# The first weight load of a decode block, issued in two parts

## Chip, cores and metric

One core of one Trainium2 chip. The metric is the device time of one execution in microseconds; the median of three runs of the kernel before is 264.27 us (264.25 to 264.36).

## The reference

One token for each of 8 sequences goes through a transformer block of width 1024, all in float32: layer norm, attention with 32 query heads on 4 key/value heads of size 128 over the last 1024 cached positions, output projection and residual; then layer norm, a gated feed-forward layer (3584 wide, gelu) and residual.

```python
def _A_ref(x, k_cache, v_cache, wq, wo):
    W = min(4096, max(256, Sk // 4))          # 1024
    q = (x @ wq).reshape(B, Sq, Hq, Dh).transpose(0, 2, 1, 3)
    k = jnp.repeat(k_cache[:, :, Sk - W:, :], rep, axis=1)
    v = jnp.repeat(v_cache[:, :, Sk - W:, :], rep, axis=1)
    p = _softmax(jnp.einsum("bhqd,bhkd->bhqk", q, k) * (Dh ** -0.5), axis=-1)
    o = jnp.einsum("bhqk,bhkd->bhqd", p, v)
    return o.transpose(0, 2, 1, 3).reshape(B, Sq, Hq * Dh) @ wo

def _B_ref(x, w_gate, w_up, w_down):
    h = _gelu(jnp.einsum("bsd,df->bsf", x, w_gate)) * jnp.einsum("bsd,df->bsf", x, w_up)
    return jnp.einsum("bsf,fd->bsd", h, w_down)

h = x + _A_ref(_layernorm(x), k_cache, v_cache, wq, wo)
h2 = h + _B_ref(_layernorm(h), w_gate, w_up, w_down)
```

## The kernel before

Weights and cache windows, 111 MB in all, lie in memory in the order of their use, each piece as 128 rows of equal length that are one contiguous stretch. They pass through two buffers in SBUF, `wbuf[0]` and `wbuf[1]`, of 128 x 16384 float32 each (64 KB a row, 8 MB a buffer). The first eleven loads fill a whole buffer in turn: two halves of wq, two of the keys, two of the values, two of wo, then gate and up. Smaller pieces follow: three of 4 MB, two of 2 MB, and a tail of 1 MB, 512 KB and two of 256 KB.

`load(k)` (its DMA is line 186) issues load k on SyncE's queue; its completion adds 16 to the semaphore of its buffer, `landed[0]` or `landed[1]`. Loads 0 and 1 are issued at the start without a wait, load 0 being the first half of wq. Between them ScalarE issues the DMA of x (line 191), 16 rows of 2 KB, which waits only for GpSimd's memset of its tile. Each later load waits until TensorE has done the last products on its buffer. The tail's four loads go through `move` (line 83).

TensorE runs a loop of stages that is written ahead of everything else. In a stage it takes the semaphore `turn` (the wait in `take` is line 127), makes eight transposes of the tile `tin` (line 132), then takes `landed[i]` and `ready[i]` and makes 32 products in two halves with the buffer's weights (line 146), the left side being the small tile `st[i]`. `turn` and `ready` are raised by the engines that make these tiles. Ahead of the loop it sets a register and branches to the stage; it waits for nothing there.

The first stage needs: x landed, the layer norm on VectorE and ScalarE (lines 221 to 233), eight transposes, two copies on VectorE (line 241), and a fill of each `st` on VectorE and GpSimd (line 246); and for its products load 0. After the last stage TensorE makes the down projection's last blocks from the tail (lines 450, 463 and 478), the result is copied (lines 482 and 483) and two DMAs carry it out.

All semaphores made through `Flow.sem` are cleared at the end by SyncE, as one range.

Of the kernel before, what the change touches and what calls it, by code (L numbers as in the profile page):

```python
# [10 lines left out]
D = 1024  # L11
# [79 lines left out]
def decode_block(nc, x, flow, tail, outs):  # L91

    fl = Flow(nc)
# [10 lines left out]
    wbuf = [space[:, i * BUF:(i + 1) * BUF] for i in range(2)]  # L104
# [7 lines left out]
    landed = [fl.sem("wa"), fl.sem("wb")]  # L112
    ready = [fl.sem("ga"), fl.sem("gb")]
    turn = fl.sem("turn")
    steps = fl.sem("steps")
    pace = fl.sem("pace")


    def pe(it, step):
# [3 lines left out]
    t = nc.tensor  # L123
# [29 lines left out]
        ins.then_inc(steps, 1)  # L153

    t.reg_mov(count, 0)
    t.br("stage")
    with nc.body("stage", valid_engines=[PE]):
        back = t.mark_branch_hint_location()
# [23 lines left out]
    def load(k, *waits):  # L182
        i, a, src, own = flow[k]
        n = src.shape[1]
        s = fl.sem(f"part{k}") if own else landed[i]
        fl.start("sync", lambda e: e.dma_start(wbuf[i][:, a:a + n], src), waits).then_inc(s, 16)
        return s, 16

    load(0)
    x_in = fl.sem("x")  # L190
    fl.start("scalar", lambda e: e.dma_start(xh[0:64:CP, :], x), [x_zero]).then_inc(x_in, 16)
    x_in = x_in, 16
# [95 lines left out]
    for hf in range(2):  # L288
# [16 lines left out]
        for k, engine in ((0, "vector"), (1, "scalar")):  # L305
            src = tp[:, k * N:(k + 1) * N].rearrange("p (c j m) -> p j c m", c=4, j=NQ)
# [7 lines left out]
    for hf in range(2):  # L314
# [17 lines left out]
        for s in range(2):  # L332
            src = tp[:, 64 * s:64 * s + 64].rearrange("p (b h) -> p h b", h=REP)
# [60 lines left out]
    for k in range(2, len(flow)):  # L394
        i, a, src, mine = flow[k]
# [37 lines left out]
    c0 = 0  # L433
# [133 lines left out]
```

## Time and profile before

| | |
|---|---|
| median of 3 runs | 264.27 us |
| the profiled execution's own time | 264.18 us |
| its span, first to last instruction | 262.9 us |
| weights' DMA queue, share of 16 engines' span | 98.3% |
| TensorE busy | 153.1 us (58%) |
| VectorE, ScalarE, GpSimd busy | 35.0, 16.5, 15.8 us |
| memory read | 111.18 MB, 423 GB/s over the span |
| x, issue to landing | 9.4 us |

The profile is one execution. All times in it are microseconds from the first instruction, so that the span is 1.3 us shorter than the time of the same execution. A DMA is cut into packets, here one for each row, shared out among 16 DMA engines; each engine ends its part of a DMA with a small write (under 512 B) to the DMA's semaphore, which the profile counts as a packet too. A packet belongs to the stretch in which it starts, with its whole duration, so that a short stretch can show more than 100% of its time.

### The profile page before, as it was taken

What the parts mean: (1) busy time and instruction counts of PE and PEld (TensorE: products, weight loads), DVE (VectorE), ACT (ScalarE), POOL (GpSimd) and SP (SyncE); (2) the same over time, 40 slices, a digit from 0 to 9 for tenths busy, and PEclk for the clock granted to TensorE, in tenths of its full rate; (3) what the DMA queues carried; (4) which work ended last, traced back from release to release, by engine and by line L of the source; (5) the groups of instructions that cost most, each with busy time, mean ns of one, the idle gap of its engine ahead of it and who ended that gap; (6) DMA issues with size and microseconds to landing.
All of it is one profiled execution on the core that took longest, in us unless ns stands there. A gap on an engine that the chain in (4) does not pass through costs nothing. (4 is left out here: it accounts for less than half of the span.)

```text
span 262.9 us, 2330 instructions
## 1 busy us (share of the span) xinstructions
PE 153.1 (58%) x992; PEld 51.6 (20%) x992; DVE 35.0 (13%) x79; ACT 16.5 (6%) x25; POOL 15.8 (6%) x31
## 2 busy tenths in 40 slices
PE   0024945816926617937728908529919509966696
PEld 0021221211211112212212202122212202312112
DVE  0220010000030110040220010730011300131012
ACT  1000000000040110000000000200200000010000
POOL 5020010010000000010020000020000200001000
PEclk9999995986995975975956995955977956999799
DMA  8998997999899899989999997999999799999995
GB/s 319 484 449 349 479 479 329 469 479 449 349 479 479 369 429 479 449 349 479 479 399 399 479 459 339 479 479 399 399 479 479 319 464 414 439 439 399 431 419 207
DMA packets 3200, 111.31 MB, mean 423 GB/s; under 512 B 368, under 2 KB 624, under 8 KB 1024
## 3 DMA queue, kind: packets, MB, share of 16 engines
q1 hardware_dynamic: 3024, 111.22, 98.3%
q10 hardware_dynamic: 176, 0.10, 0.1%
HBM read 111.18 MB, written 0.13 MB: 423 GB/s over the span
## 5 line engine op out<-in xcount | busy, mean ns | idle before, releaser
L146 PE MATMUL big<-w,st 128*32 128x512 f32 x832 | 133.9, 728 | 72.9 <-PEq L127 69.6
L146 PEld LDWEIGHTS big<-w,st 128*32 128x32 f32 x832 | 36.7, 130 | 161.9 <-issue 159.4
L132 PE MATMUL tp<-ident,tin 128*128 128x128 f32 x104 | 16.7, 312 | 34.2 <-PEq L127 34.2
L132 PEld LDWEIGHTS tp<-ident,tin 128*128 128x128 f32 x104 | 13.2, 159 | 44.5 <-issue 44.5
L255 POOL COPY st<-ot 128x256 f32<-128x256 f32 x8 | 2.9, 402 | 77.6 <-DVE ot L334 77.6
L293 DVE TENSOR_REDUCE nmax<-big 128x1 f32<-128x1024 f32 x2 | 2.4, 1224 | 29.9 <-PE big L146 29.9
L246 POOL COPY st<-xt 128x1024 f32<-128x1024 f32 x2 | 3.0, 1524 | 51.7 <-DVE xt L241 51.7
L271 DVE TENSOR_TENSOR tin<-big,q 128x512 f32<-128x512 f32 x2 | 1.4, 692 | 32.3 <-PE big L146 32.3
L319 DVE TENSOR_TENSOR o<-big,o 128x512 f32<-128x512 f32 x2 | 1.4, 692 | 30.7 <-PE big L146 30.7
L281 POOL COPY st<-qz 128x1280 f32<-128x1280 f32 x2 | 2.5, 1256 | 35.1 <-DVE qz L276 35.1
L255 POOL COPY st<-at 128x256 f32<-128x256 f32 x6 | 2.6, 466 | 31.5 <-DMA w<-weights 25.5
L270 ACT COPY q<-big 128x512 f32<-128x512 f32 x2 | 1.2, 586 | 35.5 <-PE big L146 35.5
L443 DVE TENSOR_TENSOR d<-big,d 128x512 f32<-128x512 f32 x2 | 1.4, 692 | 14.9 <-PE big L146 14.9
L405 DVE TENSOR_TENSOR gs<-big,gs 128x512 f32<-128x512 f32 x1 | 0.7, 692 | 19.1 <-PE big L146 19.1
L318 ACT COPY o<-big 128x512 f32<-128x512 f32 x2 | 1.2, 586 | 31.5 <-PE big L146 31.5
L255 POOL COPY st<-xt 128x256 f32<-128x256 f32 x2 | 1.3, 661 | 30.1 <-DVE us L377 30.1
L295 ACT ACTIVATE tin<-big,nmax 128x1024 f32<-128x1024 f32 x2 | 2.2, 1114 | 12.8 <-DVE nmax L293 12.8
L295 ACT ACT_TABLE_LOAD x1 | 1.3, 1283 | 25.1 <-DVE nmax L293 25.1
L348 DVE TENSOR_TENSOR y<-big,y 128x512 f32<-128x512 f32 x1 | 0.7, 692 | 16.1 <-PE big L146 16.1
L226 ACT ACT_TABLE_LOAD x2 | 2.6, 1283 | 1.9 <-POOL ident L197 1.9
L373 DVE TENSOR_TENSOR gs<-big,gs 128x512 f32<-128x512 f32 x1 | 0.7, 692 | 14.7 <-PE big L146 14.7
L404 ACT COPY gs<-big 128x512 f32<-128x512 f32 x1 | 0.6, 586 | 30.6 <-PE big L146 30.6
(75 smaller groups left out, 44.6 us busy)
## 6 DMA issues: line engine op xcount, KB each, us to landing
w<-weights SPq DMA_DIRECT2D x3, 4096.0 KB, 22.8
w<-weights SPq DMA_DIRECT2D x2, 2048.0 KB, 23.8
w<-weights SPq DMA_DIRECT2D x1, 1024.0 KB, 24.3
w<-weights SPq DMA_DIRECT2D x1, 512.0 KB, 25.2
w<-weights SPq DMA_DIRECT2D x2, 256.0 KB, 25.5
w<-weights SPq DMA_DIRECT2D x11, 27.3
out<-o_fin SPq DMA_DIRECT2D x1, 64.0 KB, 1.6
out<-o_fin ACTq DMA_DIRECT2D x1, 64.0 KB, 1.6
```

The lines of the kernel that those rows point to most:

```text
L132: ins = t.transpose(tp[:, i * P:(i + 1) * P], tin[:, i * P:(i + 1) * P], ident)
L146: ins = t.matmul(out[32 * j:32 * j + 32, :], st[i][:, s0:s0 + 32], wbuf[i][:, w0:w0 + N], start=(c == 0), stop=(c == 3))
L226: tok = run("scalar", lambda e: e.activation(sd, ve, AF.Sqrt), tok)
L246: fill = run(engine, lambda e: e.tensor_copy(windows(i), half.unsqueeze(2).to_broadcast([P, 2, NQ, 4 * 32])), tok, *clear)
L255: tok = run(engine, lambda e: e.tensor_copy(windows(i)[:, k, 2 * e2:2 * e2 + 2].rearrange("p h (c m) -> p h c m", m=32), s[:, e2].unsqueez ...
L270: tok = run("scalar", lambda e: e.copy(q_sb, w0), pe(0, ("a0", "b0")[hf]))
L271: tok = run("vector", lambda e: e.tensor_add(tin[:, 0:N], w1, q_sb), tok, pe(0, end), pe(0, ("t0", "t1")[hf]))
L281: fill = run("gpsimd", lambda e: e.tensor_copy(st[hf].rearrange("p (k n) -> p k n", k=2), qz[hf].unsqueeze(1).to_broadcast([P, 2, NQ * WIN ...
L293: tok = run("vector", lambda e: e.tensor_reduce(out=nmax, in_=s_ps, axis=AX.X, op=ALU.max, negate=True), pe(1, ("a1", "b1")[hf]))
L295: p_ok = run("scalar", lambda e: e.activation(tin, s_ps, AF.Exp, bias=nmax, accum_out=tot), tok, pe(1, ("t0", "t1")[hf]))
L319: tok = run("vector", lambda e: e.tensor_add(o_sb, big[hf][:, N:2 * N], o1), tok, pe(2, ("a1", "b1")[hf]))
L443: tok = run("vector", lambda e: e.tensor_add(d0, ya[:, k], d0), tok, pe(6, f"a{k}"))
```

## The change

Load 0 is issued as two DMAs on SyncE's queue. The first carries the first 1024 float32 (4 KB) of each of the 128 rows and signals a new semaphore, `first`; the second carries the other 60 KB of each row and signals `landed[0]`, as the whole load did. TensorE waits once for `first`, ahead of its branch into the stages. All else stays.

```diff
@@ -114,6 +114,7 @@
     pace = fl.sem("pace")
+    first = fl.sem("first")
@@ -153,6 +154,7 @@
     t.reg_mov(count, 0)
+    t.wait_ge(first, 16)
     t.br("stage")
@@ -186,7 +188,10 @@
-    load(0)
+
+    i, a, src, _ = flow[0]
+    for (c0, c1), s in (((0, D), first), ((D, src.shape[1]), landed[i])):
+        nc.sync.dma_start(wbuf[i][:, a + c0:a + c1], src[:, c0:c1]).then_inc(s, 16)
     x_in = fl.sem("x")
```

## Rows read from the trace of the kernel before

**Rows 1.** The page: span, busy tenths of the DMA engines in 40 slices, the weights' queue (packets, MB, share).

```profile
span 262.9 us, 2330 instructions
...
DMA  8998997999899899989999997999999799999995
...
q1 hardware_dynamic: 3024, 111.22, 98.3%
```

**Rows 2.** The chain that ended last, its end: start us, us, what.

```profile
233.38 0.33 SPq L83
...
233.76 25.23 DMA w<-weights
...
259.03 0.42 PE acc L463 x8
...
260.96 0.27 ACT o_fin L482
```

**Rows 3.** SyncE's waits (total us, times, longest); issues of loads 2 and 10.

```profile
SPq L186 <- PE big L146: 222.9, 12, 33.1
...
L186 SPq DMA_DIRECT2D w<-weights x1: 327/327/327, 34.7 to 34.7; - x1
...
L186 SPq DMA_DIRECT2D w<-weights x1: 327/327/327, 190.7 to 190.7; - x1
```

**Rows 4.** Packets starting in 41.15 to 41.68 us and 195.89 to 196.46 us.

```profile
DMA packets 32, 1.05 MB, mean 1979 GB/s; under 512 B 16, under 2 KB 16, under 8 KB 16
...
DMA packets 32, 1.05 MB, mean 1840 GB/s; under 512 B 16, under 2 KB 16, under 8 KB 16
```

**Rows 5.** The timeline of the first 24 us: start us, us, what [idle before].

```profile
0.74 0.85 SPq L186 DMA_DIRECT2D w<-weights  x2
...
1.28 0.57 ACTq L191 DMA_DIRECT2D xh<-x  x1
...
10.68 0.69 DVE L221 BATCH_NORM_STATS2 ln_bn<-xh 64x6 f32<-64x512 f32 x1 [8.60 <-DMA xh<-x]
...
14.06 1.94 PE L132 MATMUL tp<-ident,tin 128*128 128x128 f32 x8 [14.06 <-PEq L127]
...
16.59 1.56 POOL L246 COPY st<-xt 128x1024 f32<-128x1024 f32 x1 [12.50 <-DVE xt L241]
...
23.03 7.54 PE L146 MATMUL big<-w,st 128*32 128x512 f32 x40 [7.04 <-PEq L127]
```

**Rows 6.** DMA in 1.70 to 2.95 us (40 slices; queue), then 4.80 to 5.40 us.

```profile
GB/s 0 4194 6291 0 2097 8389 0 2097 2097 2097 2097 0 0 0 0 0 0 0 0 0 2097 0 0 0 0 0 0 0 0 0 0 0 0 0 0 0 0 0 0 2097
...
q1 hardware_dynamic: 16, 1.05, 245.9%
...
q1 hardware_dynamic: 16, 1.05, 403.1%
```

**Rows 7.** ScalarE's DMA queue in 7.20 to 7.80 us, then in 9.74 to 10.26 us.

```profile
q10 hardware_dynamic: 16, 0.03, 14.0%
...
q10 hardware_dynamic: 16, 0.00, 1.7%
```

**Rows 8.** The weights' queue in 100 to 117 us and in 257.22 to 257.94 us.

```profile
q1 hardware_dynamic: 112, 7.34, 99.7%
...
q1 hardware_dynamic: 71, 0.29, 100.0%
```

**Rows 9.** Packets starting in 256.66 to 257.23 us and 257.94 to 258.49 us.

```profile
DMA packets 63, 0.21 MB, mean 367 GB/s; under 512 B 16, under 2 KB 16, under 8 KB 59
...
DMA packets 105, 0.21 MB, mean 387 GB/s; under 512 B 16, under 2 KB 16, under 8 KB 105
```

**Rows 10.** Packets starting in 21.80 to 22.35 us and 259.27 to 259.83 us.

```profile
DMA packets 32, 1.05 MB, mean 1907 GB/s; under 512 B 16, under 2 KB 16, under 8 KB 16
...
DMA packets 51, 0.07 MB, mean 128 GB/s; under 512 B 16, under 2 KB 16, under 8 KB 51
```

**Rows 11.** SyncE's first two issues: count, ns min/median/max, first and last start us.

```profile
L186 SPq DMA_DIRECT2D w<-weights x2: 377/401/425, 0.7 to 1.2; - x2
```

## Prediction

> **What bounds the kernel now.** I read the page's DMA lines first. The sixteen DMA engines are busy through nearly the whole span, 98.3% of it for the weights' queue alone [rows 1]. Then I read the chain that ended last: it ends in 25.2 us of one piece, weights in transfer, and only some 2.2 us of TensorE and ScalarE work stand behind the last landings, before the output's DMA [rows 2]. So the end is the queue's first packet plus the time of all its packets plus a tail that no load can shorten. Next I asked whether the queue ever runs dry. SyncE issues each later load when TensorE has left the buffer, so these waits are long (222.9 us in all, twelve of them), yet they cost nothing: load 2 is issued at 34.7 us, while load 1's sixteen completion writes come from 41.15 us on; the tightest that I found is load 10, issued at 190.7 us, behind load 9's completion writes from 195.9 us on [rows 3, 4]. Compute thus has at least 5.2 us to spare before it can delay a transfer. It follows that this change counts only through what it does to the queue: where its stream begins, what each packet costs, and what lies between packets.
>
> **The first load before.** SyncE issues the first two loads from 0.74 us on, ScalarE issues x at 1.28 us [rows 5]. The first sixteen packets, one of 64 KB on each engine, start between 1.73 and 2.95 us; their share of 245.9% of a 1.25 us window, over 16 engines and 16 packets, is 3.07 us each. The second round gives 403.1% of 0.6 us, 2.42 us each [rows 6]. So the start costs 0.65 us per engine over the steady rate, once. x's packets begin after two rounds (7.2 to 7.8 us) and its completion writes come after a third (9.74 to 10.26 us), so the first use of x is at 10.68 us [rows 5, 7].
>
> **The change, part by part.**
>
> *The added packets.* Each engine has 8 of the 128 rows. Eight packets of 64 KB become eight of 4 KB and eight of 60 KB: the bytes stay, eight packets and one completion write are added. The price of a packet: 112 packets of 64 KB take 99.7% of 17 us on 16 engines, so 0.997 x 16 x 17 / 112 = 2.421 us each; 71 packets of 4 KB near the end take 100.0% of 0.72 us, so 16 x 0.72 / 71 = 0.162 us each [rows 8]. The difference, 2.259 us over 61,440 B, is 0.03677 ns per byte; 4 KB by that are 0.151 us, so a packet has 0.011 us of its own. Eight make 0.09 us; a completion write is 1.7% of 0.52 us on average per engine, 0.009 us [rows 7]. Sum: +0.10 us, all on the path, since the queue is never idle. The lower bound is 0.07, since packets of one engine overlap by a few nanoseconds: a whole DMA of 128 rows of 4 KB, the very shape of the added one, lies between the completion writes from 256.66 and from 257.94 us, 1.28 us, or 0.160 us a row [rows 9]. I take +0.10.
>
> *The rate of the short rows at the start.* The trace has 4 KB rows only where they were queued 25 us ahead and lie in one piece of memory. Here they are the first thing the queue does, and lie 64 KB apart. No row shows that. Bounds: at best the 0.160 us a row of [rows 9]; at worst each row pays what the first packets paid, 0.65 us [rows 6], seven more times: +4.6 us. I take the former, as the first packet's extra was gone in the second round, and as the engine has all eight descriptors of its own to read ahead. Below nothing: if the extra 0.65 us is owed to the length of the first packets, part of it can go; the engines' completion writes of the first load stand in a window of 0.55 us, and still do for the last block [rows 10], so the engine that starts last ends last, and at most about 0.5 us can be won by starting all of them like the earliest.
>
> *One more issue on SyncE.* An issue takes 0.38 to 0.43 us [rows 11]. The 60 KB rows are issued at about 1.17 us, load 1 at about 1.6 us. The first part keeps each engine busy from 1.74 us for 0.65 + 8 x 0.162 = 1.95 us, until about 3.7 us; the second part's packets, if they come 1.0 us after their issue as the first did (0.74 to 1.74 us), are there at 2.2 us. Cost nothing, covered by 1.5 us. Were this cover gone, at most the issue's 0.43 us would show. Load 1 has 20 us of cover. ScalarE's queue, which issues x, and GpSimd's are not passed by any moved step.
>
> *The wait on TensorE.* It stands ahead of the branch into the stages. Behind it on TensorE are the first eight transposes, and for them VectorE's copy of x into the stationary tile waits. The first part lands at about 3.7 us, and a landing takes some 0.4 us to be seen (x: last completion write up to 10.26, first use 10.68 us): 4.1 us. TensorE has nothing to do before 14.06 us [rows 5]. Cost nothing; if x comes early enough to lift that cover, the next cover is the load itself.
>
> *x earlier.* x is issued as before, but what stands ahead of it on each engine is now short. If it keeps its third place, it is there at about 3 us; if all short rows and two long ones stand ahead, at about 8.2 us, and seen at about 11 us. VectorE's work on x so starts between 3.5 and 11 us instead of 10.68. GpSimd's fill from it ends at 16.59 + 1.56 = 18.15 us now; the first products begin at 23.03 us, when the first load has landed [rows 5, 10]. So up to 7 us gained here meet a wait of 4.9 us that is already there: late next is the load, and it is worth 0.
>
> Sum: +0.10 us. Against the profiled execution's own time of 264.18 us (span 262.9 us and 1.3 us around it) that is 264.28; the median of the runs shown is 264.27, 0.09 above it, so I forecast **264.37 us**. About 0.2%, 0.53 us, is what a measurement of this kernel can tell from no change.
>
> **One rule against the trace.** A DMA of 128 rows of 4 KB adds 1.28 us to the queue's time and nothing between it and its neighbours [rows 9]. The Trainium skill, "DMA: Bandwidth & Descriptors", "Rules for kernel authors", asks for at least 1 MiB per DMA, and its "Anatomy of one DMA" fits a DMA by a constant of about 2.0 us plus its bytes (for the software path); the first part has 0.5 MiB. By that rule the sum would be an estimate of 264.27 + 2.0 = 266.3 us; the trace does not agree for a queue that is full.
>
> **The rivals.**
> (a) *A quicker start.* The first packets' extra 0.65 us shrinks when they are short, or the engines that start last catch up under the short rows. For it: that engine starts lie between 1.73 and 2.95 us while all must wait for the slowest. Against it: the extra looks like time until the first byte, which a shorter packet doesn't shorten. Price up to -0.51 + 0.10 = -0.41 us on its own; over the bound only where the whole 0.65 us goes too. Time 263.7 to 263.86 us. Chance of crossing -0.53: 0.11.
> (b) *Short rows that start cold* (the other side). Each of the eight rows touches a new stretch of memory, 0.16 us after the one before, where 64 KB rows gave 2.42 us of cover for it. Price 0 to 7 x 0.65 = 4.6 us; it decides from (0.53 - 0.10) / 7 = 0.06 us a row. For it: the first round is the only one that shows such a cost. Against it: none of the later rounds shows any. Time 264.9 to 268.9 us, most likely near the lower end. Chance 0.10.
> (c) *The second part starts only after the first is through*, so that a start is paid twice: the 1.0 us from issue to first packet (0.74 to 1.74 us) becomes a hole. Against it: small DMAs in a row leave no hole [rows 9]. 264.37 + 1.0 = 265.4 us. This is how the rule above would show here. Chance 0.04.
> (d) *The change does not do what it says for x:* x stays behind the long rows. The time is the forecast's.
>
> **How the numbers follow.** The forecast, with (d), and with gains and losses of (a) and (b) under the bound: 0.75; its own range is 263.9 to 264.8. Faster by more: (a), 0.11. Slower by more: (b) and (c), 0.14. The range that leaves out no more than 2 in 10 takes in most of (a) and the near end of (b): 263.75 to 265.1 us.
>
> **What the profile after would show.** Right: 3168 packets instead of 3024 in the weights' queue (128 rows and 16 completion writes more); 128 packets of 4 KB in the first 4 us; the first load's completion writes from 21.8 to 22.4 us, late by 0.1 us, and every later landing by as much; x used before 10.7 us; first products at 23.1 us; the last chain again one piece of weights. Wrong in the way of (a): those writes before 21.6 us. Wrong in the way of (b): more than 1.4 us between the first and the last start of the short rows on the engines, and all landings late by the same. Wrong in the way of (c): a hole in the DMA line between 3 and 5 us. Wrong altogether: an idle DMA queue later on, with SyncE's issue of a load behind the landing before it.

## The result

The changed kernel took 264.87 us (median of 22 runs, 264.42 to 265.33), the kernel before 264.47 us in the same runs (264.13 to 264.89): a ratio of 1.0016, 95% interval 1.0010 to 1.0022. That is +0.40 us where +0.10 was forecast: inside the range and within 0.2%, but four times the sum, and the interval does not hold the sum. The profiled execution took 264.83 us.

The profile after, the page: span, busy tenths of the DMA engines, the weights' queue.

```profile
span 263.5 us, 2332 instructions
...
DMA  9999998998999899989989997999999899999995
...
q1 hardware_dynamic: 3168, 111.22, 98.2%
```

The chain that ended last, its end (start us, us, what):

```profile
234.33 25.24 DMA w<-weights
...
259.61 0.43 PE acc L468 x8
...
261.56 0.27 ACT o_fin L487
```

The chain has the pieces and the lengths of [rows 2], all of them about 0.6 us later; the queue has the 144 packets more that were foreseen and is as full as in [rows 1]. So the loss is older than the chain. The start shows where it is. The timeline of the first 24 us:

```profile
0.74 0.85 SPq L194 DMA_DIRECT2D w<-weights  x2
...
1.28 0.57 ACTq L196 DMA_DIRECT2D xh<-x  x1
...
9.78 0.69 DVE L226 BATCH_NORM_STATS2 ln_bn<-xh 64x6 f32<-64x512 f32 x1 [7.70 <-DMA xh<-x]
...
13.15 1.94 PE L133 MATMUL tp<-ident,tin 128*128 128x128 f32 x8 [13.15 <-PEq L128]
...
23.65 1.93 PE L147 MATMUL big<-w,st 128*32 128x512 f32 x8 [8.55 <-PEq L128]
```

Against [rows 5], x is used 0.9 us earlier and the transposes come 0.9 us earlier, yet the first products come 0.6 us later: they wait for the load. Packets starting in three windows of the changed kernel, 3.60 to 4.57 us, 22.08 to 22.92 us and 259.52 to 260.41 us:

```profile
DMA packets 68, 1.13 MB, mean 1166 GB/s; under 512 B 16, under 2 KB 16, under 8 KB 52
...
DMA packets 32, 1.05 MB, mean 1248 GB/s; under 512 B 16, under 2 KB 16, under 8 KB 16
...
DMA packets 83, 0.14 MB, mean 154 GB/s; under 512 B 16, under 2 KB 16, under 8 KB 83
```

Each window holds just the sixteen completion writes (under 512 B) of one DMA: of the first part, of the rest of load 0, and of the last weights. The engines' ends of load 0 lie over 0.84 us instead of the 0.55 us of [rows 10], and the last of them comes at 22.92 instead of 22.35 us. From there to the last weights' last write it is 260.41 - 22.92 = 237.49 us; before it was 259.83 - 22.35 = 237.48 us [rows 10]. So all of the loss in this pair of executions, 0.57 us, is made before 22.92 us, and nothing after that adds to it or takes from it. The profiled execution of the kernel before (264.18 us) is one of its quicker ones: the pair's times differ by 0.65 us, the medians by 0.40.

The weights' queue of the changed kernel in 1.70 to 3.60, 3.30 to 3.60, 5.90 to 7.00, 8.30 to 9.35, 10.60 to 11.70 and 14 to 21 us:

```profile
q1 hardware_dynamic: 92, 0.38, 89.3%
...
q1 hardware_dynamic: 30, 0.12, 99.4%
...
q1 hardware_dynamic: 16, 0.98, 215.6%
...
q1 hardware_dynamic: 16, 0.98, 218.5%
...
q1 hardware_dynamic: 16, 0.98, 211.0%
...
q1 hardware_dynamic: 48, 2.95, 97.3%
```

The first 92 short rows take 0.893 x 16 x 1.9 / 92 = 0.295 us each on average. Over the 0.160 of [rows 9] that is 92 x 0.135 / 16 = 0.78 us per engine. The forecast had allowed for 0.65 us of it, what the first round before cost over the steady rate; the rest is +0.13 us. It is not a slower rate of all the short rows: those that start from 3.30 us on take 0.994 x 16 x 0.3 / 30 = 0.159 us, the price in the full queue. The earliest rows of each engine are slow. The 60 KB rows take 0.973 x 16 x 7 / 48 = 2.270 us once the stream is steady, but 2.156 x 1.1 = 2.372, 2.294 and 2.321 us in their second to fourth rounds: +0.10, +0.02 and +0.05 us. With the forecast's 0.10 us for the packets themselves, the average engine is by this sum 0.40 us later. The last engine is 0.57 us later, since the engines lie further apart.

### The profile page after: what moved, and what is told of

The parts are those of the page before. It is cut to its first block, busy times and chain, and to the rows that moved or that the text cites. A ratio compares the mean times of both kernels' runs of the same rounds, so it can differ in the third digit from the quotient of the medians.

```text
span 263.5 us, 2332 instructions
## 1 busy us (share of the span) xinstructions
PE 155.4 (59%) x992; PEld 52.8 (20%) x992; DVE 35.0 (13%) x79; ACT 16.5 (6%) x25; POOL 15.8 (6%) x31
## 3 DMA queue, kind: packets, MB, share of 16 engines
q1 hardware_dynamic: 3168, 111.22, 98.2%
## 5 line engine op out<-in xcount | busy, mean ns | idle before, releaser
L133 PE MATMUL tp<-ident,tin 128*128 128x128 f32 x104 | 17.6, 325 | 33.3 <-PEq L128 33.3
L133 PEld LDWEIGHTS tp<-ident,tin 128*128 128x128 f32 x104 | 14.0, 166 | 43.6 <-issue 43.6
## 6 DMA issues: line engine op xcount, KB each, us to landing
w<-weights SPq DMA_DIRECT2D x1, 7680.0 KB, 22.2
```

The costliest lines, as they stand in the source:

```text
L133: ins = t.transpose(tp[:, i * P:(i + 1) * P], tin[:, i * P:(i + 1) * P], ident)
```

## The experiments

Ratios are to the kernel before in the same runs, with 95% intervals. In each profile I read the same thing: the window that just holds the sixteen completion writes of load 0. They are gathered at the end of this section. Each edit is cut to its main lines. It is against the kernel before for the wait alone, the split in a full queue and the three parts, against the 8 KB kernel for 9 KB, and against the changed kernel for the others.

**The wait alone.** Theory A: short rows at the start of the queue. Rival W: the wait ahead of the branch.

```diff
     t.reg_mov(count, 0)
+    t.wait_ge(first, 1)
     t.br("stage")
...
+    go("gpsimd", first, 1, consts)
```

> The first load is whole, as before; TensorE waits ahead of its branch for GpSimd's addition at about 4.1 us, the time at which the first part was in. Theory A (the loss of 0.40 us comes from short rows at the cold start of the queue: the engines start less evenly, and the last one sets the end): 0.0 us against before, within 0.15; the first load's completion writes spread over about 0.51 us as before. Rival W (the wait ahead of the branch makes TensorE or its code late): +0.3 to +0.4 us, with the completion writes unmoved.

Measured: 264.55 us against 264.38, ratio 1.0001 (0.9991 to 1.0011). Completion writes of load 0, 21.81 to 22.29 us:

```profile
DMA packets 32, 1.05 MB, mean 2185 GB/s; under 512 B 16, under 2 KB 16, under 8 KB 16
```

The wait costs nothing that the time or the writes show; W falls.

**The split in a full queue.** Load 0 whole, load 1 split; the wait for its first part stands on GpSimd.

```diff
-    load(1)
+    for (c0, c1), s in (((0, D), first), ((D, src.shape[1]), landed[i])):
+        nc.sync.dma_start(wbuf[i][:, a + c0:a + c1], src[:, c0:c1]).then_inc(s, 16)
```

> Load 0 is whole; load 1, which lies behind it in a full queue, is issued as 4 KB and 60 KB of each row, and GpSimd waits for its first part ahead of the signal for its products. Theory A: only the packets' own cost, +0.10 us; the spread of the completion writes stays about 0.51 us and no 60 KB packet takes more than about 2.27 us. Rival N (4 KB rows 64 KB apart, or 60 KB rows that start off the 64 KB grid, are slow wherever they lie): +0.3 to +0.4 us, the same as the change.

Measured: 264.62 us against 264.38, ratio 1.0007 (0.9998 to 1.0016). Completion writes of load 0, 21.90 to 22.49 us, and of load 1's first part, 23.16 to 23.76 us:

```profile
DMA packets 53, 0.15 MB, mean 257 GB/s; under 512 B 16, under 2 KB 16, under 8 KB 53
...
DMA packets 55, 1.02 MB, mean 1700 GB/s; under 512 B 16, under 2 KB 16, under 8 KB 40
```

Eight rows of 4 KB, 64 KB apart, take 1.26 us per engine here, the 0.16 us a row of [rows 9], and the engines keep their distance. So rows 64 KB apart are not slow in themselves: N falls as to the first part's rate. The time alone (+0.18 to +0.24 us) lies between the two expectations and would not have told. One thing expected under Theory A did not come: the weights' queue in 26 to 40 us shows that the 60 KB rows take more than 2.27 us.

```profile
q1 hardware_dynamic: 97, 5.96, 98.9%
```

That is 0.989 x 16 x 14 / 97 = 2.284 us each. And load 0, which is whole here and lies ahead of the split, is in 0.14 us later than before (22.49 against 22.35 us). Why was not tried; so part of this kernel's loss lies ahead of the split.

**Two halves.** First part 32 KB of each row.

```diff
-    for (c0, c1), s in (((0, D), first), ((D, src.shape[1]), landed[i])):
+    for (c0, c1), s in (((0, 8 * D), first), ((8 * D, src.shape[1]), landed[i])):
```

> Load 0 in two parts of 32 KB of each row, the wait as in the change. Theory A: the first packets are long, so the start is like before; the packets' own cost alone, +0.10 us, spread of the completion writes 0.5 to 0.6 us. Rival L (any split of the first load, one more issue and one more completion, costs it): +0.3 to +0.4 us.

Measured: 264.56 us against 264.38, ratio 1.0003 (0.9993 to 1.0014). Completion writes of load 0, 21.69 to 22.20 us; and TensorE's first work:

```profile
DMA packets 32, 1.05 MB, mean 2056 GB/s; under 512 B 16, under 2 KB 16, under 8 KB 16
```
```profile
13.37 1.94 PE L133 MATMUL tp<-ident,tin 128*128 128x128 f32 x8 [13.37 <-PEq L128]
```

The interval reaches to +0.37 us, so the time alone leaves room for L. Load 0's writes do not: they come no later than before and lie no further apart. One more DMA and one more completion do not make the loss; L falls. Here the first part is in only at about 12.5 us, and TensorE's transposes do wait for it, though their input is there before (VectorE's copy of x ends at 11.2 us). That costs nothing, as the load comes at 22.2 us.

**The first part in one stretch of memory.** The host lays the first 4 KB of the 128 rows down as one piece of 512 KB, the other 60 KB of each as the next piece.

```diff
+    parts = [parts[0][:, 0:D], parts[0][:, D:], *parts[1:]]
...
+    srcs = [srcs[0:2], *srcs[2:]]
```

> As the change, but the first 4 KB of the 128 rows lie in memory as one contiguous piece of 512 KB, and the other 60 KB of each as the next piece. Theory A in its form 'short packets at the start, wherever they lie': +0.3 to +0.5 us as the change, spread of the first part's completion writes about 0.9 us. In its form 'each row touches a new 64 KB of memory while it is cold': +0.1 us, spread 0.5 us.

Measured: 264.24 us against 264.38, ratio 0.9988 (0.9979 to 0.9998). Completion writes of the first part, 3.31 to 3.71 us, and of the rest, 21.74 to 22.10 us; then of the last weights, 259.76 to 260.25 us:

```profile
DMA packets 46, 1.04 MB, mean 2601 GB/s; under 512 B 16, under 2 KB 16, under 8 KB 30
...
DMA packets 32, 1.05 MB, mean 2913 GB/s; under 512 B 16, under 2 KB 16, under 8 KB 16
...
DMA packets 36, 0.04 MB, mean 84 GB/s; under 512 B 16, under 2 KB 16, under 8 KB 36
```

This is quicker than either form expected. The same short packets at the same place in the queue start quicker than the whole load, by 0.25 us on the last engine, and load 0 comes 0.8 us earlier than in the changed kernel. So short first packets alone do not make the loss; where in memory they lie counts. The profiled execution took 264.81 us: from 22.10 to 260.25 us it takes 238.15 us, 0.67 more than 237.48. The second profile of this kernel loses 0.4 us in this way in mid-stream, two halves 0.35 and 16 KB rows 64 KB apart 0.2; before, the change and most others lose none. Why was not tried. These are the four profiles in which load 0 was in earliest, so no profile shows that what is won at the start reaches the end.

**The change again.**

> The changed kernel once more, beside the next three. Theory B (rows of 4 KB that lie 64 KB apart start slowly while the queue is cold; the same rows in one contiguous piece do not): +0.3 to +0.5 us against before, the first part's completion writes spread over about 0.9 us and the last of them at about 4.5 us. Rival (the loss of the first profile was a matter of that execution): +0.1 us, spread about 0.5 us.

Measured: 264.72 us against 264.46, ratio 1.0011 (1.0002 to 1.0020). First part 3.63 to 4.52 us, load 0 22.16 to 22.85 us:

```profile
DMA packets 62, 1.11 MB, mean 1243 GB/s; under 512 B 16, under 2 KB 16, under 8 KB 46
...
DMA packets 32, 1.05 MB, mean 1520 GB/s; under 512 B 16, under 2 KB 16, under 8 KB 16
```

The start is the same as in the first profile; the time, +0.26 to +0.29 us, is just under the low end of what was expected.

**Other pitches.** Rows of load 0 68 KB apart; the first part's rows 8 KB apart in a piece of their own (the rest in one stretch); then 9 KB, with the pitch alone changed (all that lies behind the piece in memory moves on by 128 KB with it).

```diff
+    src = src[:, 0:BUF]
...
+    parts[0] = np.concatenate([parts[0], parts[0][:, 0:D]], 1)
```

> As the change, but the rows of load 0 lie 68 KB apart in memory instead of 64 KB, with 4 KB between them that are not read. Theory B1 (each row touches a new, distant piece of memory while the queue is cold): as the change, +0.3 to +0.5 us. Theory B2 (it is the pitch of just 64 KB, so that all 128 short rows begin alike): as the contiguous one, -0.3 to +0.1 us, first part in by 3.8 us.

Measured: 264.45 us against 264.46, ratio 0.9998 (0.9989 to 1.0007). First part 3.42 to 4.35 us, load 0 21.72 to 22.55 us:

```profile
DMA packets 61, 1.10 MB, mean 1185 GB/s; under 512 B 16, under 2 KB 16, under 8 KB 45
...
DMA packets 32, 1.05 MB, mean 1263 GB/s; under 512 B 16, under 2 KB 16, under 8 KB 16
```

B1 falls by the time. B2 has the time right but not its sign: the first part is in by 4.35 us, not by 3.8.

```diff
+    pair = pair[0][:, 0:D], pair[1]
...
+    parts = [np.tile(parts[0][:, 0:D], 2), parts[0][:, D:], *parts[1:]]
```

> The first part's 128 rows of 4 KB lie 8 KB apart in a piece of 1 MB of their own, the other 60 KB of each row as a contiguous piece. Theory B1: the rows are near each other, so as the contiguous one, -0.3 to +0.1 us. Theory B2: as the contiguous one. Rival B3 (any gap between short rows costs, since the reads are then not one stretch): +0.3 to +0.5 us as the change.

Measured: 265.09 us against 264.46, ratio 1.0025 (1.0016 to 1.0034). First part 3.77 to 4.97 us, load 0 22.13 to 23.26 us:

```profile
DMA packets 53, 1.07 MB, mean 891 GB/s; under 512 B 16, under 2 KB 16, under 8 KB 37
...
DMA packets 32, 1.05 MB, mean 928 GB/s; under 512 B 16, under 2 KB 16, under 8 KB 16
```

Both theories expected this kernel to be as quick as the contiguous one; B1 falls again, and B2 with it: rows close together, in a megabyte, are the slowest yet. B3's loss came, larger than it expected. The 4 KB pad beside 64 KB rows had brought the time back to that of before, with the engines still 0.8 us apart. The loss here has another course than in the change. The weights' queue in 2.90 to 3.70 us holds short rows alone:

```profile
q1 hardware_dynamic: 44, 0.18, 91.1%
```

That is 0.911 x 16 x 0.8 / 44 = 0.265 us a row, where the change was back at 0.159 from 3.30 us on. With 8 KB the rows stay slow; with 64 KB only the earliest are.

```diff
-    parts = [np.tile(parts[0][:, 0:D], 2), parts[0][:, D:], *parts[1:]]
+    parts = [np.concatenate([parts[0][:, 0:D], parts[0][:, 0:D + 256]], 1), parts[0][:, D:], *parts[1:]]
```

> The first part's rows of 4 KB lie 9 KB apart in a piece of their own, the rest contiguous: the kernel with 8 KB, with one number changed and a larger gap. Theory C (at the queue's start the engines read in step, and a pitch of a power of two makes their reads collide; 68 KB cost less than 64 KB, 8 KB most): -0.2 to +0.2 us, load 0's last completion write by 22.5 us. Rival B3 (any gap between short rows costs): +0.5 to +0.8 us, load 0's last completion write near 23.2 us, as with 8 KB.

Measured: 264.39 us against 264.33, ratio 0.9999 (0.9990 to 1.0008). First part 3.60 to 4.16 us, load 0 21.81 to 22.36 us:

```profile
DMA packets 51, 1.00 MB, mean 1792 GB/s; under 512 B 16, under 2 KB 16, under 8 KB 36
...
DMA packets 31, 0.98 MB, mean 1787 GB/s; under 512 B 16, under 2 KB 16, under 8 KB 16
```

From 8 to 9 KB, load 0 comes 0.9 us earlier and the time falls by 0.26%. A gap between short rows is not what costs (B3 falls); its size is. C expected this outcome; that the reads collide was not measured. The two kernels ran on different chips, each beside the kernel before on its own (264.46 and 264.33 us). The contiguous kernel, which ran on both, differs by 0.17 us in load 0's last write and by 0.0011 in its ratio, much less than this pair.

**A longer first part.** 16 KB of each row, rows 64 KB apart; then the same 16 KB in one stretch.

```diff
-    for (c0, c1), s in (((0, D), first), ((D, src.shape[1]), landed[i])):
+    for (c0, c1), s in (((0, 4 * D), first), ((4 * D, src.shape[1]), landed[i])):
```

> As the change, with 16 KB of each row in the first part and 48 KB in the second, all within rows 64 KB apart. Theory B: each row has 0.6 us of transfer to cover the start of the next one, so the loss is between the packets' own cost and the change's: +0.1 to +0.25 us, spread of the first part's completion writes 0.5 to 0.7 us. Rival (the loss belongs to the split with a small first part as such, or to its second part's start off the 64 KB grid): +0.4 us.

Measured: 264.28 us against 264.46, ratio 0.9993 (0.9984 to 1.0002); load 0 21.82 to 22.14 us:

```profile
DMA packets 32, 1.05 MB, mean 3277 GB/s; under 512 B 16, under 2 KB 16, under 8 KB 16
```

It came out better than any theory expected: no loss at all, with the engines only 0.32 us apart.

```diff
-    parts = [parts[0][:, 0:D], parts[0][:, D:], *parts[1:]]
+    parts = [parts[0][:, 0:4096], parts[0][:, 4096:], *parts[1:]]
```

> The first part is 16 KB of each row, as one contiguous piece of 2 MB, the second 48 KB of each as the next piece. If contiguous memory is what makes the start quick, -0.2 to -0.4 us and load 0's last completion write at 22.0 to 22.1 us; if it is the short first packets in contiguous memory, the start lies between that of the whole load (22.3 us) and of the 4 KB piece (22.09 us), -0.2 to 0.0 us.

Measured: 264.66 us against 264.33, ratio 1.0012 (1.0003 to 1.0021); load 0 21.96 to 22.74 us:

```profile
DMA packets 32, 1.05 MB, mean 1344 GB/s; under 512 B 16, under 2 KB 16, under 8 KB 16
```

A miss for both expectations. One stretch of memory is no cure: 16 KB rows lie 16 KB apart in it, and the start is nearly as slow as in the change; the same rows 64 KB apart are quick. This pair, too, ran on two chips, the quick one on that of the 8 KB kernel. The first part's writes, 7.32 to 7.64 us with rows 64 KB apart and 7.46 to 8.24 us in one stretch, already show the whole difference:

```profile
DMA packets 32, 0.79 MB, mean 2458 GB/s; under 512 B 16, under 2 KB 16, under 8 KB 16
...
DMA packets 34, 0.82 MB, mean 1050 GB/s; under 512 B 16, under 2 KB 16, under 8 KB 16
```

**A contiguous piece ahead of the short rows.** Three parts: 4 KB contiguous, then 4 KB from rows 64 KB apart, then 56 KB.

```diff
+    for (c0, c1), src, s in (((0, D), pair[0], first), ((D, 2 * D), pair[1][:, 0:D], first),
+                             ((2 * D, BUF), pair[1][:, D:BUF - D], landed[i])):
```

> Three parts: 4 KB of each row as one contiguous piece, then 4 KB of each row from rows 64 KB apart, then the other 56 KB from those rows. Theory D (rows 64 KB apart cost only what stands first in a cold queue; in a queue that runs, as where load 1 was split, nothing): the contiguous part takes the start, so -0.3 to 0.0 us and load 0's last completion write at 22.1 to 22.3 us. Rival (the collision of short rows 64 KB apart needs only engines that are in step, and they still are after 2 us): +0.2 to +0.5 us, 22.5 us or later.

Measured: 265.20 us against 264.33 (five runs), ratio 1.0034 (1.0021 to 1.0048). Completion writes of the three parts, 3.45 to 3.78, 4.70 to 5.23 (with fifteen of x's) and 21.83 to 23.49 us:

```profile
DMA packets 49, 0.14 MB, mean 410 GB/s; under 512 B 16, under 2 KB 16, under 8 KB 49
...
DMA packets 69, 0.82 MB, mean 1538 GB/s; under 512 B 31, under 2 KB 31, under 8 KB 56
...
DMA packets 32, 1.05 MB, mean 632 GB/s; under 512 B 16, under 2 KB 16, under 8 KB 16
```

Theory D is missed by 0.9 us; the loss is in the rival's direction and larger than the rival expected. Of D only this came: the second part, 64 KB apart, takes 1.25 to 1.45 us after the first, near the 1.28 of a full queue. But then the engines lose step in the long rows, from 0.53 to 1.66 us apart. So the loss is not bound to the first packets; it came in later rounds too, as in the 60 KB rows of the change.

**The contiguous one again.**

> The contiguous first part of 4 KB once more. All theories: -0.1 to -0.4 us against before, load 0's last completion write at 22.0 to 22.2 us.

Measured: 264.50 us against 264.33, ratio 0.9999 (0.9990 to 1.0009); load 0 21.64 to 22.27 us:

```profile
DMA packets 32, 1.05 MB, mean 1665 GB/s; under 512 B 16, under 2 KB 16, under 8 KB 16
```

A miss, if a small one: the time is unchanged, where all theories expected a gain, and the last write is at 22.27, not by 22.2 us. The kernel is quicker than the change both times, but quicker than the kernel before only once: that it beats it is not shown.

**All of them, in the order of load 0's last completion write:**

| kernel | load 0's writes, us | ratio |
|---|---|---|
| 4 KB contiguous | 21.74 to 22.10 | 0.9988 |
| 16 KB, 64 KB apart | 21.82 to 22.14 | 0.9993 |
| two halves | 21.69 to 22.20 | 1.0003 |
| 4 KB contiguous, again | 21.64 to 22.27 | 0.9999 |
| wait alone | 21.81 to 22.29 | 1.0001 |
| before | 21.80 to 22.35 | 1 |
| 4 KB, 9 KB apart | 21.81 to 22.36 | 0.9999 |
| load 1 split | 21.90 to 22.49 | 1.0007 |
| 4 KB, 68 KB apart | 21.72 to 22.55 | 0.9998 |
| 16 KB contiguous | 21.96 to 22.74 | 1.0012 |
| the change, again | 22.16 to 22.85 | 1.0011 |
| the change | 22.08 to 22.92 | 1.0016 |
| 4 KB, 8 KB apart | 22.13 to 23.26 | 1.0025 |
| three parts | 21.83 to 23.49 | 1.0034 |

The writes are of one execution each, the ratios of all runs. Three kernels that issue load 0 whole (before, wait alone, load 1 split) differ by 0.20 us in its last write, so the order of close neighbours says nothing. What stands out is the last five: load 0's last write at 22.74 us or later, and the only ratios above 1 whose intervals leave out 1. That a late last engine at load 0 goes with a longer time is the finding. In the pairs where the layout alone changes the time, the last engine is late already when the first part is in: the change and 4 KB contiguous, 4.57 against 3.71 us (load 0: 22.92 and 22.10); 8 and 9 KB, 4.97 against 4.16 us (23.26 and 22.36).

## Why the prediction was right, and where it was not

*What bounds it*: right. The queue stays full, and what the change loses at the start arrives at the end undiminished (237.48 and 237.49 us from load 0 to the last weights). But that the time lies in the range is in part luck: the forecast's own range ended at 264.8 us, 264.87 lies in the piece that was added for the near end of (b), and the sum missed three quarters of the loss. Of the 0.50 us between the forecast and 264.87, 0.20 is the kernel before, which took 264.47 in these runs and not 264.27. Of the signs named for being right, the 3168 packets and the earlier x came; load 0's writes from 21.8 to 22.4 us (measured 22.08 to 22.92) and first products at 23.1 us (23.65) did not.

*The packets' own cost, +0.10 us*: consistent with the runs, not measured by itself. A split inside the full queue gave 1.0007, two halves 1.0003, both with intervals that hold +0.10 us (1.0004); eight short rows in the full queue took 1.26 us, as summed. In the changed kernel's steady stream a short and a long row take 0.159 + 2.270 = 2.429 us, 0.008 more than the 2.421 of a whole row: 0.06 us for eight, a little under the forecast.

*SyncE's extra issue and the wait on TensorE, nothing*: right. The wait alone gave 1.0001, and where it did hold up the transposes, in the two halves, 1.0003 (0.9993 to 1.0014).

*x earlier, worth nothing*: right. It was used at 9.78 us, inside the 3.5 to 11 that were given and near their late end, and the load was late next.

*The rate of the short rows at the start*: this is the step that failed. I took 0.160 us a row, the row's price in the full queue, after one first packet that costs 0.65 us more, because that extra was gone in the second round and an engine can read ahead. With it the first 92 rows would have taken 0.162 + 16 x 0.65 / 92 = 0.275 us each; they took 0.295. The extra was not gone after one packet: it was 0.78 us an engine, +0.13 us more than forecast. A loss in these rows was named as rival (b), at a chance of 0.10 to pass 0.2%; it came, under that bound. The sign given for (b), starts more than 1.4 us apart on the engines, did not: the first part's ends lie over 0.97 us. The reason given for (b) was not the right one either. Rows that touch distant memory one after another are not slow as such: rows 8 KB apart were worse than rows 64 KB apart, and rows 9 KB apart cost nothing.

*Two terms were missing*: the first rounds of the long rows, +0.17 us, and the engines' spread, from 0.55 to 0.84 us. The prediction did say that the engine that starts last ends last, but used it only for what could be won. It prices losses too: in the profiled pair the last engine's +0.57 us is what the end shows, while the mean engine's is +0.40. That the medians also differ by 0.40 us is no check of the mean; the executions of the kernel before spread over 0.76 us.

*The rule on DMA sizes*: the measured +0.40 us is far from the estimate of +2.0 us that was made from the constant in the Trainium skill, "DMA: Bandwidth & Descriptors", "Anatomy of one DMA"; and the kernel with a first DMA of the same 0.5 MiB in one stretch (4 KB contiguous) lost nothing.

What stays open is why one layout starts evenly and another does not. That the layout of the first part's rows counts is shown on one chip by 4 KB rows in one stretch, 8 KB apart and 64 KB apart (0.9988, 1.0025, 1.0011). That it is their pitch rests on 8 against 9 KB, and on 16 KB rows at 16 against 64 KB; in both pairs the chip changed too, and with the pitch the place in memory of what follows or the pitch of the second part. These were not tried apart. That powers of two are to blame is only argued, and there are counterexamples: 4 KB rows at 4 KB, and 16 KB rows at 64 KB, are powers of two and quick.

## What to carry to other kernels

Where DMA queues are full from the first packet to the last, look at the spread of the engines' completion writes of the first load: here the last engine set the end, and what it lost in the first microseconds was not won back in any profile. A packet price read from the full queue did not hold for the first rounds; price the start from a start, and take the last engine, not the mean. Splitting the first load bought nothing, since its consumer needs all of it, though x behind it got in 0.9 us earlier.

## What was not expected of the hardware

Moving 128 rows of 4 KB from 8 KB to 9 KB apart, at the head of the queue, went with 0.26% of the kernel's time: load 0's last write moved from 23.26 to 22.36 us (on two chips, as said above). The same 16 KB rows were in by 22.14 us when they lay 64 KB apart, and by 22.74 us when they lay in one stretch. In a full queue, rows of 4 KB at 64 KB took 1.26 us per engine, no more than contiguous ones.
